# Loading half of q over SyncE's queue in fp32 at the start of a pooled-attention and gated-projection kernel

## The chip, the core and the metric

The kernel runs on one core of a Trainium2 chip. The metric is the time of one execution on the device in microseconds (us), as the median of several executions. The traces used here are of one profiled execution of each kernel; their span runs from the first to the last instruction and is some 1.8 us shorter than the time. All times in the text without another origin are counted from the start of that span.

## The reference

```python
# q, k, v: [8, 8, 576, 64] fp32 (batch, head, token, depth)
k_p = k.reshape(B, H, Sp, 8, D).mean(axis=3)           # 576 keys pooled to 72
v_p = v.reshape(B, H, Sp, 8, D).mean(axis=3)
attn = softmax(q @ k_p.transpose(0, 1, 3, 2) / sqrt(D))
x = (attn @ v_p).transpose(0, 2, 1, 3).reshape(4608, 512)
h = x @ w_in                                           # [512, 2048]
out = (h * cos(h)) @ w_out                             # [2048, 512]
```

## The kernel before

The two big products run in nine chunks of 512 tokens, and attention of the later batches is woven into them. Only batch 0 has nothing to hide under: its k, q and v must be loaded, pooled on TensorE (a product with a 0/1 matrix called `groups`), transposed, and go through softmax, before the first big product can start. The start looks like this (cut):

```python
warm = consts.tile([128, 512], BF16, name="warm")
nc.vector.memset(warm, 1.0)
...
# half of k in fp32 over SyncE's queue, cast by ScalarE; the rest over GpSimd's queue, which casts as it loads
nc.sync.dma_start(out=k_first..., in_=even_view(k, 0, 0, 2))
nc.scalar.copy(out=staged["k", 0][:, 0:2]..., in_=k_first)
load_even(staged["q", 0], 0, q, 0, 2)          # GpSimd's queue: first half of q
... # GpSimd: index fills
load_even(staged["k", 0], 0, k, 2, 4)
load_even(staged["q", 0], 0, q, 2, 4)
load_even(staged["v", 0], 0, v)
make_identity(nc, identity)
... # VectorE: groups; then GpSimd: the weights, batch 1, w_out piece by piece

warm_up(10, obanks[0])                          # products that only keep TensorE's clock up
pool_k_mm(0, obanks[1], 0, 2)(vec)              # pool k's first half, VectorE copies it to kk
warm_up(2, banks[1][:, 0, :])
puts = q_transpose_mm(0, banks[2][:, 0, :], 0, 5), q_transpose_mm(0, obanks[0], 5, 9)
puts[0](vec)
puts[1](act)
warm_up(2, banks[1][:, 0, :])
scores(0, us[0], banks[0])
scores(0, us[1], banks[1])
... # second half of k and q, scores, v, sums and products with v
up_mm(0, 0, 0, 2)                               # first big product
```

Three moments carry the argument. The *first scores* need pooled k and transposed q. The *last scaled product* is the last of four by which VectorE finishes batch 0; TensorE's big products run without a gap from then on. And the *second piece* of w_out must have landed when TensorE comes to it at about 38 us.

The softmax here doesn't subtract the row's maximum and nothing guards it: scores larger than these inputs give would overflow.

## Time and profile before

The median of three executions was 303.98 us (303.52 to 304.59).

| moment, before | us |
|---|---|
| q's first half landed (issued from 1.26) | 7.05 |
| TensorE at full clock from | 6.51 |
| first scores start | 8.80 |
| last scaled product of batch 0 starts | 18.24 |
| second piece of w_out lands | 38.06 |
| TensorE takes it up, after a wait of 0.46 | 38.10 |
| last copy of a whole output tile (128x512) by VectorE | 294.88 |
| span | 302.1 |

In a line of the timeline the first two numbers are the start and the busy time in us; a bracket at the end gives how long the engine was idle before, and what ended that. In the chain of waits a line is start, duration, and what the end of the program was waiting for at that time. In the stretches, each engine has its busy time and, in brackets, its instructions, in the order PE, PEld, DVE, ACT, POOL; then come the granted TensorE clock (1.00 is full), the DMA share and GB/s written.

### The profile page before, as it was taken

Reading aid. Unit: us, or ns where it says so; the run is one execution under the profiler, and the core shown is the slowest. Engines: PE = TensorE matmul, PEld = TensorE weight load, DVE = VectorE, ACT = ScalarE, POOL = GpSimd, SP = SyncE. Lnnn points to the kernel's source line nnn. Section 1 sums busy time; section 2 is a strip of 40 time slices with the busy share of each in tenths; the row PEclk is TensorE's granted clock in tenths of the full one; section 3 lists DMA queues with packets and bytes.
Section 4 is the critical chain, followed back from the end, with each engine's and each line's share of the span. In section 5 each row is a group of like instructions: output and inputs, shape, how many; then the busy total and the mean of one; then the engine's idle time right before and its main releaser. Section 6 shows DMA issues by size and latency. Waiting matters only on the chain.

```text
span 302.1 us, 4605 instructions
## 1 busy us (share of the span) xinstructions
PE 294.0 (97%) x1798; PEld 141.6 (47%) x1798; DVE 172.3 (57%) x211; ACT 206.8 (68%) x255; POOL 129.8 (43%) x92
## 2 busy tenths in 40 slices
PE   8799999999999999999999999999999999999995
PEld 3545544445544454455444544454444544444444
DVE  5558636574566366645675566656574567425712
ACT  3887897469856986688768876788578956606500
POOL 8553007984973596349733991399100000000000
PEclk9999999999999999999999999999999999999999
DMA  7999999639546943695169617881900330131032
GB/s 152 201 207 206 208 204 196 152 44 174 109 113 105 167 92 70 123 171 113 44 132 161 115 36 162 129 141 36 167 5 1 71 69 0 27 79 35 0 71 71
DMA packets 44006, 32.92 MB, mean 109 GB/s; under 512 B 22096, under 2 KB 39248, under 8 KB 43984
## 3 DMA queue, kind: packets, MB, share of 16 engines
q0 software_dynamic: 19744, 18.07, 38.2%
q1 hardware_dynamic: 24080, 14.42, 21.0%
q8 instruction: 14, 0.23, 0.3%
q10 hardware_dynamic: 160, 0.13, 0.2%
q14 instruction: 8, 0.07, 0.1%
HBM read 36.70 MB, written 9.44 MB: 153 GB/s over the span
## 4 chain that ended last, share of the span: by engine, by line
PE 85%; DMA 10%; POOL 2%; ACT 1%; issue 0%; DVE 0%; POOLq 0%; ACTq 0%
PE obank L310 39%; PE bank L297 37%; DMA w_out_sb<-in_moe_w_out_dram 6%; PE bank L241 5%; DMA w_in_sb<-in_moe_w_in_dram 4%; PE bank L211 3%; PE bank L328 1%; POOL kv_st L84 1%; POOL kp L384 1%; POOL q_b L84 1%; ACT L285 0%; ACT cos L304 0%; ACT ex L218 0%; POOL identity masks.py:197 0%; DVE o_sb L316 0%
## 5 line engine op out<-in xcount | busy, mean ns | idle before, releaser
L310 PE MATMUL obank<-w_out_sb,g_sb 128*128 128x512 bf16 x560 | 132.5, 380 | 0.5 <-DMA w_out_sb<-in_moe_w_out_dram 0.5
L297 PE MATMUL bank<-xT,w_in_sb 128*128 128x512 bf16 x576 | 126.5, 379 | 0.0
L304 ACT ACTIVATE cos<-bank,half_pi 128x1024 f32<-128x1024 f32 x72 | 80.0, 1113 | 63.3 <-PE bank L297 63.3
L307 DVE TENSOR_TENSOR g_sb<-bank,cos 128x1024 bf16<-128x1024 f32 x72 | 88.1, 1225 | 48.2 <-ACT cos L304 48.2
L297 PEld LDWEIGHTS <-w_in_sb 128*128 128x128 bf16 x576 | 55.5, 98 | 68.6 <-DVE xT L252 2.5
L310 PEld LDWEIGHTS <-g_sb 128*128 128x128 bf16 x560 | 52.2, 97 | 56.9 <-issue 3.7
L252 DVE TENSOR_TENSOR xT<-bank,inv 64x512 bf16<-64x512 f32 (+1 forms) x72 | 45.3, 629 | 50.1 <-ACT inv L248 49.2
L141 POOL TENSOR_TENSOR kv_st<-kv_st 72x2048 f32<-72x2048 bf16 x12 | 48.7, 4056 | 35.2 <-DMA kv_st<-in_k_dram 35.2
L247 ACT ACTIVATE lnc<-bank 64x512 f32<-64x512 f32 (+1 forms) x72 | 39.2, 544 | 2.9 <-PE bank L241 1.3
L218 ACT ACTIVATE ex<-bank 72x1024 bf16<-72x1024 f32 (+1 forms) x40 | 35.0, 928 | 5.3 <-PE bank L211 5.2
L316 DVE COPY o_sb<-obank 128x512 f32<-128x512 f32 x35 | 23.6, 689 | 16.8 <-PE obank L310 16.2
L142 POOL TENSOR_TENSOR kv_st<-kv_st 72x1024 f32<-72x1024 f32 x12 | 28.2, 2348 | 1.0
L248 ACT ACTIVATE inv<-lnc 128x512 f32<-128x512 f32 (+1 forms) x36 | 21.0, 583 | 1.1
L241 PE MATMUL bank<-ex,vz 72*128 72x256 bf16 (+1 forms) x176 | 20.0, 243 | 0.2 <-ACT ex L218 0.2
L241 PEld LDWEIGHTS <-vz 72*128 72x128 bf16 x176 | 13.7, 97 | 9.9 <-issue 0.6
L145 POOL TENSOR_TENSOR kp<-kv_st 72x512 bf16<-72x512 f32 x12 | 14.9, 1264 | 0.5
L211 PE MATMUL bank<-qT,kk 64*72 64x256 bf16 (+1 forms) x192 | 13.3, 252 | 1.1 <-ACT qT L193 0.5
L211 PEld LDWEIGHTS <-kk 64*72 64x72 bf16 x192 | 7.6, 110 | 11.9 <-issue 8.1
L285 ACT ACT_TABLE_LOAD x9 | 11.5, 1283 | 0.9 <-PEq L515 0.7
L288 ACT ACT_TABLE_LOAD x9 | 11.5, 1283 | 0.2
L495 POOL COPY gate<-kk 1x1 bf16<-1x1 bf16 x5 | 0.9, 180 | 24.7 <-DMA kk<-kp 24.7
L84 POOL DMA_DIRECT2D q_b<-in_q_dram x10 | 7.7, 773 | 2.7 <-DMA w_in_sb<-in_moe_w_in_dram 1.4
(55 smaller groups left out, 89.8 us busy)
## 6 DMA issues: line engine op xcount, KB each, us to landing
out_dram<-o_sb SPq DMA_DIRECT2D x70, 128.0 KB, 2.4
kv_st<-in_v_dram POOLq DMA_DIRECT2D x8, 576.0 KB, 13.0
kv_st<-in_k_dram POOLq DMA_DIRECT2D x7, 576.0 KB, 7.7
q_b<-in_q_dram POOLq DMA_DIRECT2D x6, 576.0 KB, 9.9
w_in_sb<-in_moe_w_in_dram POOLq DMA_DIRECT2D x4, 512.0 KB, 13.7
w_out_sb<-in_moe_w_out_dram POOLq DMA_DIRECT2D x4, 512.0 KB, 18.4
q_b<-in_q_dram POOLq DMA_DIRECT2D x4, 288.0 KB, 12.1
g_sb<-in_k_dram SPq DMA_DIRECT2D x1, 576.0 KB, 3.5
```

Source lines behind the costliest of these rows:

```text
L141: add(out=s, in0=x[:, :, 0:4, :], in1=x[:, :, 4:8, :], op=ADD)
L142: add(out=s[:, :, 0:2, :], in0=s[:, :, 0:2, :], in1=s[:, :, 2:4, :], op=ADD)
L211: nc.tensor.matmul(pair[:Sp, bank, c:c + n].rearrange("p (g n) -> p g n", n=64), lhsT=kk[b % 2][half[r], h0 + i, 0:Sp], rhs=att["qT", b][h ...
L218: nc.scalar.activation(out=ex[:, 0:nh * n].rearrange("p (a n) -> p a n", a=2), in_=pair[:Sp, :, 0:nh * n // 2], func=ACTF.Exp, scale=scale ...
L241: nc.tensor.matmul(pair[:, hp, (i // 2) * n:(i // 2 + 1) * n], lhsT=vz[b % 2][:, pj, 2 * hp:2 * hp + 2, :].rearrange("p a d -> p (a d)"), ...
L247: nc.scalar.activation(out=lnc[half[1 - hp]], in_=pair[half[1 - hp], hp, 0:w], func=ACTF.Ln)
L252: nc.vector.tensor_mul(out=x_out(b, u, half[hp]), in0=cols(pair[half[hp], hp, :], u), in1=cols(inv[half[1 - hp]], u))
L297: nc.tensor.matmul(h[:, j, :], lhsT=w_in_sb[fc // 4][:, ki, (fc % 4) * 128:(fc % 4 + 1) * 128], rhs=xT[:, ki, t * TILE:(t + 1) * TILE], st ...
L304: nc.scalar.activation(out=cos, in_=h, func=ACTF.Sin, bias=half_pi[:, :1])
L307: nc.vector.tensor_mul(out=g_sb[:, 2 * fp:2 * fp + 2, :], in0=h, in1=cos)
L310: nc.tensor.matmul(o, lhsT=g_sb[:, fc, ms * 128:(ms + 1) * 128], rhs=w_out_sb[fc // 4][:, fc % 4, :], start=(fc == 0), stop=(fc == FFCH - 1))
L316: nc.vector.tensor_copy(out=o[:, 0:n], in_=ps)
```

## The change

The intent is to feed batch 0 sooner. k's half comes in two loads, one per pair of heads, so that its cast starts on the first. q's half goes the same way over SyncE's queue in fp32, instead of over GpSimd's queue, and VectorE casts it. v comes in two loads, pooled and copied apart. Each product gets a PSUM bank tile of its own, so that the copies out can be shared between VectorE and ScalarE. The warm-up tile is smaller, and there are eight first warm-ups, not ten. The core of the diff (the pooling functions that take a list of banks, and batch 1's matching calls, are cut):

```diff
-    warm = consts.tile([128, 512], BF16, name="warm")
+    warm = consts.tile([128, 128], BF16, name="warm")
...
-    k_first = g_sb...[:, 0:2 * ROW * D]
-    nc.sync.dma_start(out=k_first..., in_=even_view(k, 0, 0, 2))
-    nc.scalar.copy(out=staged["k", 0][:, 0:2]..., in_=k_first)
-    load_even(staged["q", 0], 0, q, 0, 2)
+    for i, (which, src) in enumerate((("k", k), ("q", q))):
+        for j in range(2):
+            first[which, j] = g_sb...[:, (2 * i + j) * n:(2 * i + j + 1) * n]
+            nc.sync.dma_start(out=first[which, j], in_=even_view(src, 0, j, j + 1)...)
+    for j in range(2):
+        cast_first("k", nc.scalar.copy, j)
...
-    load_even(staged["v", 0], 0, v)
+    load_even(staged["v", 0], 0, v, 0, 2)
+    load_even(staged["v", 0], 0, v, 2, 4)
...
-    warm_up(10, obanks[0])
-    pool_k_mm(0, obanks[1], 0, 2)(vec)
-    warm_up(2, banks[1][:, 0, :])
+    warm_up(8, obanks[0])
+    puts = pool_k_mm(0, obanks, 0, 2)
+    for j in range(2):
+        cast_first("q", vec, j)
+    puts[0](act)
+    puts[1](vec)
+    warm_up(1, banks[2][:, 0, :])
...
+    for put in pool_k_mm(0, [banks[1][:, i, :] for i in range(2)], 2, 4):
+        put(vec)
     sums_first(0, us[1], obanks[1])
+    for put in [q_transpose_mm(0, banks[0][:, i, :], 9 + 5 * i, 14 + 4 * i) for i in range(2)]:
+        put(vec)
+    pool_v_mm(0, obanks, 0, 2)
+    scores(0, us[2], banks[2])
+    scores(0, us[3], banks[1])
+    values_then(0, us[0], obanks[0])
+    values_then(0, us[1], obanks[1])
+    pool_v_mm(0, (banks[0][:, 0, :], banks[0][:, 1, :]), 2, 4)
+    sums_first(0, us[2], banks[2][:, 0, :])
+    sums_first(0, us[3], banks[1][:, 0, :])
```

More of the change, by code (lines that the diff above doesn't have):

```diff
@@ L126, in v_part @@
         return vz[b % 2][:, :, 0:4:3, :]
-    def put_kk(b, ps, pj0, pj1, copy):
-        dst = kk[b % 2].rearrange("p (j a) n -> p j a n", a=2)
-        for a in range(2):
-            for r in range(2):
-                copy(out=dst[half[r], pj0:pj1, a, 0:Sp], in_=ps[half[a]])
     def pool_add(b, which):
@@ L148, in pool_add, with pool_k_mm, put, go @@
             add(out=v_part(b), in0=s[..., 0, :], in1=s[..., 1, :], op=ADD)
-    def pool_k_mm(b, bank, pj0, pj1):
+    def pool_k_mm(b, ps, pj0, pj1):
         kb = staged["k", b]
-        ps = bank[:, 0:(pj1 - pj0) * Sp].rearrange("p (j n) -> p j n", n=Sp)
+        ps = [p[half[a], 0:(pj1 - pj0) * Sp].rearrange("p (j n) -> p j n", n=Sp) for a, p in enumerate(ps)]
         for pj in range(pj0, pj1):
             for t in range(ROW):
-                for rows in half:
-                    nc.tensor.matmul(ps[rows, pj - pj0, :], lhsT=kb[rows, pj, t, :], rhs=groups[rows, t, :],
+                for a in range(2):
+                    nc.tensor.matmul(ps[a][:, pj - pj0, :], lhsT=kb[half[a], pj, t, :], rhs=groups[half[a], t, :],
                                      start=(t == 0), stop=(t == ROW - 1))
-        return lambda copy: put_kk(b, ps, pj0, pj1, copy)
-    def pool_v_mm(b, pair):
+        dst = kk[b % 2].rearrange("p (j a) n -> p j a n", a=2)
+        def put(a):
+            def go(copy):
+                for r in range(2):
+                    copy(out=dst[half[r], pj0:pj1, a, 0:Sp], in_=ps[a])
+            return go
+        return put(0), put(1)
+    def pool_v_mm(b, ps, pj0=0, pj1=KCH):
         vb = staged["v", b]
+        ps = [p[:Sp, 0:(pj1 - pj0) * D] for p in ps]
         for t in range(ROW):
             for hp, rows in enumerate(half):
-                nc.tensor.matmul(pair[:Sp, hp, 0:KCH * D], lhsT=groups[rows, t, :], rhs=vb[rows, :, t, :],
+                nc.tensor.matmul(ps[hp], lhsT=groups[rows, t, :], rhs=vb[rows, pj0:pj1, t, :],
                                  start=(t == 0), stop=(t == ROW - 1))
-        nc.vector.tensor_copy(out=v_part(b).rearrange("p j a d -> p a j d"),
-                              in_=pair[:Sp, :, 0:KCH * D].rearrange("p a (j d) -> p a j d", j=KCH))
+        for hp in range(2):
+            nc.vector.tensor_copy(out=v_part(b)[:, pj0:pj1, hp, :], in_=ps[hp].rearrange("p (j d) -> p j d", d=D))
     def k_transpose(b):
@@ L340, with cast_first @@
     q_tile(0)
-    k_first = g_sb.rearrange("p f n -> p (f n)").bitcast(FP32)[:, 0:2 * ROW * D]
-    nc.sync.dma_start(out=k_first.rearrange("p (j n) -> p j n", j=2), in_=even_view(k, 0, 0, 2))
-    nc.scalar.copy(out=staged["k", 0][:, 0:2].rearrange("p j t d -> p (j t d)"), in_=k_first)
-    load_even(staged["q", 0], 0, q, 0, 2)
+    first = {}
+    n = ROW * D
+    for i, (which, src) in enumerate((("k", k), ("q", q))):
+        for j in range(2):
+            first[which, j] = g_sb.rearrange("p f n -> p (f n)").bitcast(FP32)[:, (2 * i + j) * n:(2 * i + j + 1) * n]
+            nc.sync.dma_start(out=first[which, j], in_=even_view(src, 0, j, j + 1).rearrange("p j n -> p (j n)"))
+    def cast_first(which, copy, j):
+        copy(out=staged[which, 0][:, j].rearrange("p t d -> p (t d)"), in_=first[which, j])
+    for j in range(2):
+        cast_first("k", nc.scalar.copy, j)
     row_of = consts.tile([128, ROW], FP32, name="row_of")
@@ L360 @@
     groups = consts.tile([128, ROW, Sp], BF16, name="groups")
-    nc.vector.tensor_tensor(out=dist, in0=row_of.unsqueeze(2).to_broadcast([128, ROW, Sp]),
-                            in1=first_of.unsqueeze(1).to_broadcast([128, ROW, Sp]), op=mybir.AluOpType.subtract)
-    nc.vector.scalar_tensor_tensor(out=sign, in0=dist, scalar=1.0 - POOL, in1=dist, op0=ADD,
-                                   op1=mybir.AluOpType.mult)
-    nc.vector.tensor_scalar(out=groups, in0=sign, scalar1=0.0, scalar2=None, op0=mybir.AluOpType.is_le)
     nc.vector.memset(vz[0], float(POOL))
@@ L371 @@
     nc.vector.memset(half_pi, math.pi / 2.0)
+    nc.vector.tensor_tensor(out=dist, in0=row_of.unsqueeze(2).to_broadcast([128, ROW, Sp]),
+                            in1=first_of.unsqueeze(1).to_broadcast([128, ROW, Sp]), op=mybir.AluOpType.subtract)
+    nc.vector.scalar_tensor_tensor(out=sign, in0=dist, scalar=1.0 - POOL, in1=dist, op0=ADD,
+                                   op1=mybir.AluOpType.mult)
+    nc.vector.tensor_scalar(out=groups, in0=sign, scalar1=0.0, scalar2=None, op0=mybir.AluOpType.is_le)
     kv_even_tiles(1)
@@ L382 @@
     load_even(staged["v", 1], 1, v)
+    nc.gpsimd.memset(vz[1], float(POOL))
     for i in range(2):
@@ L390, in warm_up @@
         for i in range(n):
-            nc.tensor.matmul(bank, lhsT=warm[:, 0:128], rhs=warm)
+            nc.tensor.matmul(bank.rearrange("p (a n) -> p a n", a=4), lhsT=warm,
+                             rhs=warm.unsqueeze(1).to_broadcast([128, 4, 128]))
     vec, act = nc.vector.tensor_copy, nc.scalar.copy
     us = BY_HEADS
-    warm_up(10, obanks[0])
-    pool_k_mm(0, obanks[1], 0, 2)(vec)
-    warm_up(2, banks[1][:, 0, :])
-    puts = q_transpose_mm(0, banks[2][:, 0, :], 0, 5), q_transpose_mm(0, obanks[0], 5, 9)
+    warm_up(8, obanks[0])
[5 more added lines that the diff above has]
+    warm_up(1, banks[2][:, 0, :])
+    puts = q_transpose_mm(0, banks[1][:, 0, :], 0, 5), q_transpose_mm(0, banks[0][:, 0, :], 5, 9)
     puts[0](vec)
     puts[1](act)
-    warm_up(2, banks[1][:, 0, :])
-    scores(0, us[0], banks[0])
-    scores(0, us[1], banks[1])
-    pool_k_mm(0, obanks[1], 2, 4)(vec)
-    sums_first(0, us[0], banks[0][:, 0, :])
-    puts = q_transpose_mm(0, banks[2][:, 0, :], 9, 14), q_transpose_mm(0, obanks[0], 14, 18)
-    puts[0](vec)
-    puts[1](act)
-    sums_first(0, us[1], obanks[1])
-    scores(0, us[2], banks[0])
-    scores(0, us[3], banks[2])
-    nc.vector.memset(vz[1], float(POOL))
-    pool_v_mm(0, banks[1])
-    sums_first(0, us[2], obanks[0])
-    values_then(0, us[0], obanks[1])
-    values_then(0, us[1], banks[1][:, 0, :])
-    sums_first(0, us[3], banks[2][:, 0, :])
-    values_then(0, us[2], obanks[1])
-    values_then(0, us[3], obanks[0])
+    warm_up(2, banks[2][:, 0, :])
+    scores(0, us[0], banks[2])
+    scores(0, us[1], banks[0])
+    sums_first(0, us[0], obanks[0])
+    for put in pool_k_mm(0, [banks[1][:, i, :] for i in range(2)], 2, 4):
+        put(vec)
+    sums_first(0, us[1], obanks[1])
+    for put in [q_transpose_mm(0, banks[0][:, i, :], 9 + 5 * i, 14 + 4 * i) for i in range(2)]:
[8 more added lines that the diff above has]
+    sums_first(0, us[3], banks[1][:, 0, :])
+    values_then(0, us[2], obanks[0])
+    values_then(0, us[3], obanks[1])
     up_mm(0, 0, 0, 2)
@@ L431 @@
                 if fp == 4:
-                    puts = pool_k_mm(1, obanks[0], 0, 2), pool_k_mm(1, obanks[1], 2, 4)
+                    puts = pool_k_mm(1, obanks, 0, 4)
                 elif fp in (5, 6):
@@ L464 @@
         if t == 0:
-            fill[1:] = [(2, S_(0, 0)), (8, lambda: pool_v_mm(1, banks[1])), (8, lambda: values(t, REST, banks[2])),
+            fill[1:] = [(2, S_(0, 0)), (8, lambda: pool_v_mm(1, [banks[1][:, i, :] for i in range(2)])), (8, lambda: values(t, REST, banks[2])),
                         (11, S_(1, 0)), (13, V_(0, 1)), (18, S_(2, 2)), (21, V_(1, 0, later)), (26, S_(3, 1)),
```

## The prediction

> **What bounds the kernel now.** I read four views in this order: the page (busy shares, slices, the chain by engine), the chain of waits in order of time for the first 60 us, the timeline of the first 20 us, and the stretches by microsecond. The page first:
>
> ```profile
> PE 294.0 (97%) x1798; PEld 141.6 (47%) x1798; DVE 172.3 (57%) x211; ACT 206.8 (68%) x255; POOL 129.8 (43%) x92
> ...
> PE   8799999999999999999999999999999999999995
> ...
> GB/s 152 201 207 206 208 204 196 152 44 174 109 113 105 167 92 70 123 171 113 44 132 161 115 36 162 129 141 36 167 5 1 71 69 0 27 79 35 0 71 71
> ...
> PE 85%; DMA 10%; POOL 2%; ACT 1%; issue 0%; DVE 0%; POOLq 0%; ACTq 0%
> ```
>
> TensorE is busy 97% of the span and carries 85% of the chain; only the first two of the 40 slices (15 us) are short of 9 tenths before the end. The change touches batch 0 and, slightly, batch 1's product in chunk 0, so it can win no more than what is lost at the start. But DMA holds 10% of the chain, and the transfers run flat out at some 207 GB/s from slice 1 to slice 5 (38 us). So where do these DMA pieces lie? The chain in order of time:
>
> ```profile
> 5.81 10.94 DMA w_in_sb<-in_moe_w_in_dram
> ...
> 19.62 18.43 DMA w_out_sb<-in_moe_w_out_dram
> 38.06 0.04 issue
> 38.10 0.81 PE obank L310 x3
> ```
>
> From 5.81 to 38.06 us the chain is not batch 0's work at all: it is the weights in GpSimd's queue. A piece of the second projection's weights, issued at 19.62, lands at 38.06, and TensorE waits for it. From 38.10 on the chain is TensorE alone. The timeline shows how small that wait is, and the beginning and end of batch 0:
>
> ```profile
> 1.26 0.87 POOL L84 DMA_DIRECT2D q_b<-in_q_dram  x1 [0.81 <-POOLq L515]
> 1.47 4.45 PE L391 MATMUL obank<-warm 128*128 128x512 bf16 x10 [1.47 <-DVE warm L336]
> 4.30 1.15 ACT L343 CAST kv_st<-g_sb 128x1152 bf16<-128x1152 f32 x1 [2.27 <-DMA g_sb<-in_k_dram]
> 5.84 1.06 PE L157 MATMUL obank<-groups,kv_st 64*64 64x72 bf16 x36
> 8.80 0.63 PE L211 MATMUL bank<-qT,kk 64*72 64x256 bf16 x8 [0.43 <-DVE qT L193]
> 13.86 1.91 ACT L218 ACTIVATE ex<-bank 72x1024 bf16<-72x1024 f32 x2
> 18.24 0.69 DVE L282 TENSOR_TENSOR xT<-obank,inv 128x512 bf16<-128x512 f32 x1 [0.50 <-ACT inv L271]
> 38.10 0.81 PE L310 MATMUL obank<-w_out_sb,g_sb 128*128 128x512 bf16 x3 [0.46 <-DMA w_out_sb<-in_moe_w_out_dram]
> ```
>
> So batch 0's scores start at 8.80, its last product is scaled until 18.93, TensorE is then dense, and at 38.10 it has lost 0.46 us to the weights. The stretches by microsecond show the transfers starting badly (last column GB/s, before it the DMA share):
>
> ```profile
> 3.00:4.00 1.00, 1.00 (x3) 0.29 (x2) 0.96 (x2) 0.00 (x0) 1.00 (x2) 1.00 1.12 327
> 4.00:5.00 1.00, 1.00 (x4) 0.43 (x3) 0.96 (x2) 0.70 (x1) 1.00 (x2) 1.00 0.82 97
> 5.00:6.00 1.00, 1.00 (x9) 0.16 (x9) 0.84 (x2) 0.45 (x1) 0.93 (x4) 1.00 1.11 167
> 6.00:7.00 1.00, 1.00 (x37) 0.90 (x36) 0.56 (x4) 0.00 (x0) 1.00 (x2) 1.00 1.19 182
> 7.00:8.00 1.00, 1.00 (x13) 0.69 (x11) 0.94 (x4) 0.02 (x1) 1.00 (x2) 1.00 1.12 179
> 8.00:9.00 1.00, 0.57 (x6) 0.30 (x6) 0.72 (x2) 0.57 (x1) 1.00 (x3) 1.00 1.16 179
> ```
>
> SyncE's fp32 load of k runs in 2 to 4 us; then it is over, and GpSimd's queue, whose casting loads write half of what they read, comes up slowly: 97, 167, 182, 179, 179 against 207 later. That is 110+40+25+28+28 = 231 KB written short, or 231/207 = 1.1 us of transfer time lost. This, not the engines' work, sets when the weights land.
>
> **What the Trainium skill says.** "DMA: Bandwidth & Descriptors", section "Issuing engines are not separate DMA queues": all queues feed the same 16 engines and interleave, and several issuers save only issue time. The trace agrees as far as it goes: one queue alone holds the share above 1. The same page, "Latency and other measured facts", gives the first byte after about 600 ns on the hardware path and about 1 us on GpSimd's. In the packet records SyncE's load issued at 0.75 to 1.21 sends its first packet at 1.86, 0.65 us after the issue; GpSimd's, issued at 1.26 to 2.13, at 3.74, 1.6 us after. So SyncE agrees and GpSimd is slower than the page. "TensorE: Matmul & The Clock Gate", section "What's actually happening": the array runs at half clock until it has been busy for about 3.4 us; here the ten warm-up products cost 4.45/10 = 0.445 us each, and four later ones 0.60/2 = 0.30 or less. "PSUM — Partial Sum Buffer", section "PSUM bank collisions raise a hardware error": engines must be kept apart by bank and quadrant. That is the reason for a bank tile per product; no collision was allowed before either, so it buys independence of the two copies, not speed of the products.
>
> **The change part by part.**
>
> *Start of TensorE.* The warm-up tile shrinks from 128x512 to 128x128: its fill, 0.48 us, falls to about 0.15, so warm-up starts near 1.15 instead of 1.47. Eight at 0.445 take 3.6: done near 4.75. The two halves of k land near 3.5 and 4.3, and each casts on ScalarE in about 1.15/2 = 0.6: done at 4.1 and 4.9. The group matrix needs three VectorE operations (0.83+0.83+0.74 = 2.4 us); a fill of v's tile now stands before them, but GpSimd's index fills come first by 0.8 us, so they run 2.2 to 4.65. Pooling k's first half starts near 4.8, not 5.84: 1.0 us won, unless the array is still at half clock, which doubles 1.06 us and gives most of it back.
>
> *q's first half.* Two fp32 loads on SyncE behind k, 256 packets at k's pace (0.59 MB at some 390 GB/s = 1.5 us), shared with GpSimd's queue from about 4.2: landing near 5.4 and 6.4. Two new casts on VectorE of 128x576; by the 745 ns of the group compare on 648 elements, about 0.66 each: done near 6.1 and 7.05. Then VectorE's share of the copies of pooled k falls from four (1.28 us) to two (0.65), as ScalarE does the other two: done at 7.7, and the copy of q's transpose (0.49) at 8.2. Scores start near 8.2 against 8.80: 0.6 won. The casts eat 0.4 of the 1.0.
>
> *Rest of batch 0.* ScalarE is the bound from 9.25 to 18.21, with hardly a gap. One 0.57 us copy of q's transpose goes to VectorE. But the second two heads' pairs now wait on VectorE: four copies of k (1.26) and two of q's transpose (0.49+0.43) after a pooling which ends near 10.7: 10.7+2.2 = 12.9, scores 12.95, exponentials from 13.3 instead of 13.86. Four operations of normalising follow as before; the last scaled product is ready at about 18.4, not 18.93. v in two halves lies under this: half the columns, same 18 products a half, and two short copies instead of one of 0.69. **TensorE's gain at the start: 0.5 us.**
>
> *The transfers.* Bytes read are the same. A fp32 packet of SyncE (2304 B) takes 93 ns in the records; a casting one (1152 B written) takes 107, but these overlap by a share of 1.2, so about 89 each; 256 packets over 16 engines differ by 16 x 4 ns, under 0.1 us. What is won is that q's packets fill 4.0 to 5.6 us, where 110+30 KB are missing (0.7 us). Against it GpSimd's first load is issued after the index fills, some 0.6 us later, so part of its slow start moves to 5 to 9 us. **Net about 0.6 us earlier for every later landing.** GpSimd's extra fill (0.91 us, ahead of the second piece of those weights) delays an issue, not the landing: that piece waits 18.4 us behind some six others.
>
> *Sum at the wait of 38.10.* TensorE arrives at 37.64-0.5 = 37.1; the weights at 38.06-0.6 = 37.45. It starts at 37.5: 0.6 won. The next two pieces landed at 40.60 and 43.10 (18.4 and 18.1 us after issues at 22.16 and 24.96) against needs near 40.9 and 43.5; both move alike and stay just in time. After that TensorE alone counts and nothing has changed. The gain is the smaller of 0.5+0.46 (TensorE) and about 0.6 (transfers): 303.98-0.6 = 303.4; I say 303.3, as the transfers' gain could reach 1.1.
>
> **The rivals.**
>
> 1. *Full gain at the start.* If all 1.0 us of the earlier pooling reached the end, and the DMA followed, 302.9. For it: the chain's first 6 us. Against: the casts on VectorE, and the wait at 38.10.
> 2. *Transfers not advanced.* If GpSimd's slow start only moves later, the weights still land at 38.06 and TensorE waits 0.9 us instead of 0.46: 304.0, nothing won. For it: GpSimd's rate is below 207 up to 9 us whatever SyncE does, and its first load starts later.
> 3. *Harm.* SyncE's packets delay GpSimd's loads of k and q for the other heads, or the array is cold after eight warm-ups; scores slip 0.5 to 1 us: but the 0.46 of slack absorbs half: 304.5.
>
> I give these 25, 25 and 10%, and the central story 40.
>
> **Range and chances.** The rivals span 302.9 to 304.5, and the three runs of before spread over 1.1 us. Range 302.4 to 304.3. 2% is 6.1 us, three times what is lost between 1.5 and 19 us by any count above, so faster by over 2% has 1%, slower 1%, within 98%.
>
> **What would show each step.** Warm-up's start (1.15), first pooling (4.8), first scores (8.2), last scaled product of batch 0 (18.4), DMA rate at 4 to 6 us (over 200), landing of the second piece of the second weights (37.45) and TensorE's wait before it (0.3 to 0.5). If scores come a microsecond early and the end doesn't, rival 2 holds and the landing will still be 38. If the landing moves by over 1 us, I undersized the transfers. A slot of TensorE idle after 50 us that wasn't there before would prove me wrong: I take that phase as unchanged.

## The result, and the profile after

The changed kernel took 308.16, 308.17, 308.92 and 308.45 us, median 308.31; the kernel before took 303.98, 304.59, 303.52 and 303.52 in the same rounds, median 303.75. The ratio is 1.0149, with a 95% interval of 1.0124 to 1.0174. That is inside the 2% called the same, but clear: 4.6 us slower, and outside the predicted range. (A ratio here compares mean times of the same rounds, so it is not quite the ratio of the medians.)

From the page of the changed kernel, the share of TensorE and its clock in 40 slices of 7.7 us, and the chain by engine:

```profile
PE   6599999999999999999999999999999999999994
...
PEclk9589999999999999999999999999999999999999
...
PE 92%; DMA 2%; ACT 2%; issue 1%; DVE 1%; SPq 0%; ACTq 0%
```

Before, the first two digits of PE were 8 and 7. Now the second slice has 5 of TensorE and also 5 of its clock. The chain has lost most of its DMA, 10% to 2%, so the wait for the weights is not what sets the end any more. What the chain now runs through at the start is this:

```profile
2.14 7.41 DMA g_sb<-in_q_dram
9.57 0.47 DVE q_b L355
...
10.09 0.71 PE bank L197 x5
...
12.27 1.03 ACT ex L223
...
22.85 0.70 DVE xT L287
23.59 7.10 PE bank L302 x32
```

Everything waits for a load of q that SyncE began to issue at 2.14 and that landed at 9.54. It was predicted at 6.4. The timeline answers the lines that the prediction showed of before:

```profile
1.07 3.59 PE L407 MATMUL obank<-warm 128*128 128x512 bf16 x8 [1.07 <-DVE warm L341]
...
4.59 0.96 PE L152 MATMUL obank<-groups,kv_st 64*64 64x72 bf16 x36
...
6.61 0.46 DVE L355 CAST q_b<-g_sb 128x576 bf16<-128x576 f32 x1 [2.30 <-DMA g_sb<-in_q_dram]
7.13 0.40 PE L197 MATMUL bank<-identity,q_b 128*128 128x128 bf16 x4 [1.26 <-DVE q_b L355]
...
9.57 0.46 DVE L355 CAST q_b<-g_sb 128x576 bf16<-128x576 f32 x1 [2.50 <-DMA g_sb<-in_q_dram]
10.09 0.71 PE L197 MATMUL bank<-identity,q_b 128*128 128x128 bf16 x5 [2.56 <-DVE q_b L355]
...
11.58 1.07 PE L216 MATMUL bank<-qT,kk 64*72 64x256 bf16 x8
...
22.85 0.69 DVE L287 TENSOR_TENSOR xT<-obank,inv 128x512 bf16<-128x512 f32 x1 [0.60 <-ACT inv L276]
...
42.08 0.81 PE L315 MATMUL obank<-w_out_sb,g_sb 128*128 128x512 bf16 x3
```

The reader should see four things. The warm-up and the pooling of k start early, as planned (1.07 and 4.59). The second cast of q waits 2.50 us for its load, and TensorE 2.56 us behind it. The eight products of the first scores take 1.07 us where they took 0.63 before: the clock. And the product at 42.08 has no bracket: the weights had long been there.

The stretches of two microseconds show the hole and the clock that follows it:

```profile
6.00:8.00 2.00, 0.40 (x4) 0.23 (x4) 0.46 (x1) 0.15 (x1) 2.00 (x3) 1.00 1.02 199
8.00:10.00 2.00, 0.00 (x0) 0.00 (x0) 0.43 (x1) 0.00 (x0) 0.47 (x2) 0.52 1.17 199
10.00:12.00 2.00, 1.91 (x11) 1.04 (x13) 1.14 (x4) 0.58 (x1) 1.10 (x2) 0.50 1.21 205
```

TensorE works 0.40 us of the 4 us from 6 to 10. In the records its clock is full from 4.67 to 8.08, half from 8.08 to 18.32, and full from there to the end of the work. Meanwhile the transfers are not idle (199 GB/s), so I asked whose packets they are. The packets of each queue, in 4.5 to 7.5 us of the changed kernel (q0 is GpSimd's, q1 SyncE's; packets, MB written, share of 16 engines):

```profile
q0 software_dynamic: 277, 0.31, 77.0%
q1 hardware_dynamic: 135, 0.27, 27.0%
```

The same in 8 to 10 us of the changed kernel:

```profile
q0 software_dynamic: 335, 0.37, 111.9%
q1 hardware_dynamic: 18, 0.03, 4.9%
```

And in 4.5 to 7.5 us of the kernel before, where GpSimd's queue was alone:

```profile
q0 software_dynamic: 448, 0.49, 107.1%
```

While SyncE's queue had the engines to itself, from 2.0 to 4.3 us, it moved 365 packets. GpSimd's first packet is recorded at 4.31. After that SyncE's packets come at 135 in 3 us, and the last 18 trickle in between 8 and 10 us beside 335 of GpSimd's. SyncE's queue slowed when GpSimd's packets appeared at 4.31 (194 of its packets in 3 to 4 us, 25 in 5 to 6), not when GpSimd began to issue its loads at 1.42. The two queues together made 412 packets from 4.5 to 7.5, against 448 of GpSimd's queue before; but there GpSimd's queue had started 0.57 us earlier (3.74). Counted for 3 us from GpSimd's first packet, it is 421 packets of both queues in the changed kernel (156 of them SyncE's) and 402 in the kernel before (25). So in these two traces the two queues together do not move fewer packets than one; what changed is whose packets go.

The moments side by side, with four of the experiments that follow:

| | before | after | filled clock | fills first | identity first | fills, reordered |
|---|---|---|---|---|---|---|
| first half of q complete | 7.05 | 9.54 | 10.21 | 6.74 | 6.74 | 5.97 |
| first scores start | 8.80 | 11.58 | 11.93 | 8.46 | 8.46 | 7.69 |
| last scaled product starts | 18.24 | 22.85 | 21.69 | 18.22 | 18.22 | 18.69 |
| from scores to there | 9.44 | 11.27 | 9.76 | 9.76 | 9.76 | 11.00 |
| second piece of w_out lands | 38.06 | 38.11 | 39.51 | 38.40 | 37.88 | 37.69 |
| TensorE takes it up | 38.10 | 42.08 | 40.92 | 38.44 | 37.92 | 37.93 |
| of that, wait | 0.46 | 0 | 0 | 0.82 | 0.30 | 0 |
| last copy of a whole output tile | 294.88 | 298.88 | 297.74 | 295.24 | 294.72 | 294.74 |
| span | 302.1 | 306.4 | 305.2 | 302.7 | 302.2 | 302.2 |

All copies of finished output tiles, from the first at 44.84 against 48.82 to the last, lie 3.98 to 4.01 us later than before. So all of this arises before the first copy, and the long dense part is unchanged; some 0.3 us more come after the last copy.

### The profile page after: what moved, and what is told of

The parts are those of the page before. It is cut to its first block, busy times and chain, and to the rows that moved or that the text cites. A ratio compares the mean times of both kernels' runs of the same rounds, so it can differ in the third digit from the quotient of the medians.

```text
span 306.4 us, 4647 instructions
## 1 busy us (share of the span) xinstructions
PE 296.0 (97%) x1813; PEld 143.1 (47%) x1813; DVE 171.3 (56%) x213; ACT 206.8 (68%) x255; POOL 130.6 (43%) x93
## 3 DMA queue, kind: packets, MB, share of 16 engines
HBM read 36.70 MB, written 9.44 MB: 151 GB/s over the span
## 4 chain that ended last, share of the span: by engine, by line
PE 92%; DMA 2%; ACT 2%; issue 1%; DVE 1%; SPq 0%; ACTq 0%
PE bank L302 40%; PE obank L315 39%; PE bank L246 5%; PE bank L216 4%; DMA g_sb<-in_q_dram 2%; PE bank L333 1%; ACT ex L223 1%; PE bank L197 1%; PE obank L152 0%; ACT L290 0%; ACT inv L276 0%; SPq L352 0%; PE bank L152 0%; ACT lnc L275 0%; PE obank L271 0%
## 5 line engine op out<-in xcount | busy, mean ns | idle before, releaser
L290 ACT ACT_TABLE_LOAD x9 | 11.5, 1283 | 0.9 <-PEq L536 0.7
L293 ACT ACT_TABLE_LOAD x9 | 11.5, 1283 | 0.2
L103 POOL DMA_DIRECT2D kv_st<-in_v_dram x6 | 5.1, 842 | 12.7 <-PE bank L170 12.7
```

## The experiments

The first theory: q's second load is late because GpSimd's packets share the 16 engines with it, and the idle time this makes costs TensorE its clock on top. The rivals: the place of the load in SyncE's queue or its splitting is to blame; or the new compute order and the bank tiles are; or the warm-up is too short. A fourth question is why the change would not have gained even with q in time. Twelve kernels ran, all with correct results, on four chips; each call timed the kernel before on the same chip.

One thing disturbs the intervals. Some executions of the kernel before take 307.1 to 307.7 us with a mean clock of 0.983 to 0.989: 3 of 7 on the first chip, 2 of 11 on the second, none of 11 on the third (one of 305.15) and 1 of 11 on the fourth. They are not marked as slow, as none is 1.5% above the fastest, and they widen the ratios.

### q's half back on GpSimd's queue

```diff
-    for i, (which, src) in enumerate((("k", k), ("q", q))):
+    for i, (which, src) in enumerate((("k", k),)):
...
+    load_even(staged["q", 0], 0, q, 0, 2)
...
-    for j in range(2):
-        cast_first("q", vec, j)
```

> The change with one part undone: the first half of q goes back to GpSimd's casting queue, first in it, ahead of the index fills; the two casts on VectorE go. Theory A (the whole loss is q's second fp32 load, which landed at 9.54 us instead of the predicted 6.4): q lands near 7.0 as in the kernel before, the scores start near 8.1 instead of 11.58, the end is at 303.0 to 303.8 us. Rival B (the loss is in the reordered products and copies, or in v's two loads): 306 us or more though q lands early.

Measured: 304.10, 304.49, 304.45, 303.68, median 304.28; before in the same rounds 303.57 to 304.3 in four executions and 307.14 to 307.73 in three; ratio 0.9972 (0.9898 to 1.0045). q's half landed at 7.41, the first scores started at 9.38, and the last scaled product at 19.16. So this one part of the change, q's path, holds nearly the whole loss of the time: with all the rest in place the kernel is back within some 0.5 us of the four shorter executions of before. The scores are still 0.58 later than before; here q's half landed 0.36 later, eight warm-ups ended 0.68 us before `groups` was ready, the clock was full only from 9.46, and pooling took 1.29 us instead of the 0.96 of the changed kernel. The wait of 0.46 us for the weights absorbed most of that.

### Warm-up products over the wait

```diff
-    warm_up(1, banks[2][:, 0, :])
+    warm_up(18, banks[2][:, 0, :])
```

> The changed kernel with 18 warm-up products instead of 1 between the pooling of k and the transposes of q, so that TensorE is busy while it waits for q and its clock should not fall to half. The loads are untouched: q's second half should land near 9.5 as in the changed kernel. Theory C (a part of the 4.0 us is the half clock from 8.1 to 18.3): scores near 10.9, last scaled product near 21.2 instead of 22.85, end near 306.7 (1.3 to 1.8 less than the changed kernel's 308.3). Rival D (the record of the clock is not to be trusted, as one of the four timed runs shows 1.0 at the same span): no gain, 308.3 within 0.3.

Measured: 307.02, 306.25, 306.73, 307.01, median 306.87; ratio 1.0053 (0.9965 to 1.0142). The clock was full from 4.13 us on. From the timeline of this kernel:

```profile
11.93 0.63 PE L216 MATMUL bank<-qT,kk 64*72 64x256 bf16 x8 [0.30 <-DVE qT L198]
...
21.69 0.69 DVE L287 TENSOR_TENSOR xT<-obank,inv 128x512 bf16<-128x512 f32 x1 [0.60 <-ACT inv L276]
```

The scores take 0.63 us again, and the way from the scores to the last scaled product is 21.69 - 11.93 = 9.76 us, against 22.85 - 11.58 = 11.27 with half the clock. So the half clock cost 1.5 us of that way. q's loads landed late here too (8.64 and 10.21), so the lateness does not come from what TensorE does. This kernel is still some 3 us behind before: the load is the larger part.

### GpSimd's fills ahead of its loads

```diff
+    nc.gpsimd.memset(vz[1], float(POOL))
+    identity = consts.tile([128, 128], BF16, name="identity")
+    make_identity(nc, identity)
     load_even(staged["k", 0], 0, k, 2, 4)      # first of GpSimd's loads
```

> The changed kernel with GpSimd's fills (v's tile of batch 1 and the identity, about 1.4 us) ahead of its first load instead of behind, so that its queue begins near 5.7 us instead of 4.31, when SyncE's four loads should be through. Theory E (SyncE's packets are crowded out once GpSimd's queue is filled): q's two loads land near 4.8 and 5.4, scores start near 8.0, and the weights land later by up to 1 us: end 303.6 to 304.8. Rival F (SyncE's fourth load is late on its own, whatever GpSimd does): q's second half lands at 9 us or later, the end is 308 or more.

Measured: 304.54, 304.15, 304.03, 305.17, median 304.35; ratio 0.9981 (0.9907 to 1.0056). Nothing on SyncE's side was touched; GpSimd's first load was only issued at 3.02 instead of 1.42. From the timeline:

```profile
3.02 0.88 POOL L84 DMA_DIRECT2D kv_st<-in_k_dram  x1
...
6.05 0.46 DVE L355 CAST q_b<-g_sb 128x576 bf16<-128x576 f32 x1 [1.74 <-DMA g_sb<-in_q_dram]
6.76 0.46 DVE L355 CAST q_b<-g_sb 128x576 bf16<-128x576 f32 x1 [0.26 <-DMA g_sb<-in_q_dram]
8.46 0.63 PE L216 MATMUL bank<-qT,kk 64*72 64x256 bf16 x8 [0.30 <-DVE qT L198]
```

q landed at 6.03 and 6.74, 2.80 us earlier than in the changed kernel, and the clock stayed full. This is the clearest run: the same loads in the same queue land that much earlier when GpSimd issues its first load 1.6 us later (its first packet came at 5.11 instead of 4.31). The last scaled product began at 18.22, 0.02 before that of the kernel before. But the second piece of w_out landed 0.34 later (38.40), so TensorE waited 0.82 us for it, and nothing was won.

### The compute part of the change alone

```diff
-        for j in range(2):
-            first[which, j] = ...
-            nc.sync.dma_start(out=first[which, j], ...)
+        k_first = ...
+        nc.sync.dma_start(out=k_first..., in_=even_view(k, 0, 0, 2))
...
-    load_even(staged["v", 0], 0, v, 0, 2)
-    load_even(staged["v", 0], 0, v, 2, 4)
+    load_even(staged["v", 0], 0, v)
```

(against the first experiment: k and v too are loaded as before)

> The change without any of its loads: k's half in one load and one cast, q's half on GpSimd first, v in one load, as in the kernel before; the products in bank tiles of their own, the order of the products, the smaller warm-up tile and the moved fills stay. If the compute part is worth something by itself: scores near 8.2, end 303.2 to 303.7 (the weights land at 38.06 as before and hold the gain to 0.46). If it is harmful: 304.5 or more.

Measured: 304.31, 304.41, 304.57, 304.18, median 304.36; ratio 0.9978 (0.9905 to 1.0051). Scores at 9.46, last scaled product at 19.31, TensorE at the weights at 38.55. It stands as the first experiment does, 0.1 us behind: the halves of k and v make no difference that can be seen, and the compute part does not do the harm.

### Only the identity ahead of the loads

```diff
+    identity = consts.tile([128, 128], BF16, name="identity")
+    make_identity(nc, identity)
     load_even(staged["k", 0], 0, k, 2, 4)
```

> The changed kernel with only the identity's two fills (about 0.55 us) moved ahead of GpSimd's first load: a small dose of the run with all fills first (1.6 us, q landed at 6.03 and 6.74). GpSimd's queue should send its first packet near 4.85 instead of 4.31. If SyncE's packets are crowded out from the moment GpSimd's queue sends, what is left of them at that moment shrinks from 165 of 576 to about 105, and q's second half lands between, near 8.0 us, the end between 304.4 and 307.5. If there is a threshold instead (the queue late on its own, or only by the identity): 9.0 or later, or 6.8.

Measured: 304.01 and 304.45; before 303.40 to 304.08 in nine executions and 307.37 and 307.38 in two; ratio 0.9992 (0.9908 to 1.0075). I had meant this as a half dose of the delay, and it was not one. From the timeline:

```profile
1.65 1.41 POOL masks.py:199 TENSOR_SCALAR_AFFINE_SELECT identity<-identity 128x128 bf16<-128x128 bf16 x1
3.01 0.88 POOL L84 DMA_DIRECT2D kv_st<-in_k_dram  x1
```

The select took 1.41 us here, beside VectorE's work, and 0.29 us in its old place (why, no run shows), so the load left at 3.01, as in the run above. The landings of q and the start of the scores are the same to 0.01 us (6.03 and 6.74, 8.46), which confirms that run with one fill less. With the weights at 37.88 instead of 38.40, the span was 302.2, against 302.1 before.

### q's second load from ScalarE

```diff
+            issuer = nc.scalar if (which, j) == ("q", 1) else nc.sync
-            nc.sync.dma_start(out=first[which, j], ...)
+            issuer.dma_start(out=first[which, j], ...)
```

> The changed kernel with q's second half-load issued on ScalarE's queue, behind its table load, at about the same time (2.0 us) as on SyncE's. If the second half is late because it stands fourth in SyncE's queue (rival G), it lands by 7 us now, and q's first half by 6. If every packet of the hardware queues is crowded out once GpSimd's queue sends (theory E), a second hardware queue helps only by its own share of turns: it lands near 7.5 to 8.5. If that share does not exist, at 9 or later.

Measured: 307.60 and 305.92; ratio 1.0075 (0.9988 to 1.0162). The rival was that the fourth place in SyncE's queue is what is late. The views of transfers by issue (KB, us from issue to landing):

```profile
g_sb<-in_q_dram ACTq DMA_DIRECT2D x1, 288.0 KB, 3.4
...
g_sb<-in_q_dram SPq DMA_DIRECT2D x1, 288.0 KB, 6.8
```

ScalarE issued its load at 0.79, earlier than I had expected (2.0), and it landed at 4.22. But now q's first half, the last in SyncE's queue, was the late one, at 8.50. Scores at 10.96, the clock half from 7.13 to 17.37, the last scaled product at 22.23. Three of four loads got out before GpSimd's packets; whichever came last paid. So this load is not special. Nor is it simply the amount still to come when GpSimd's packets start that decides. From GpSimd's first packet on, SyncE's queue had 74 packets left here, and its last load landed at 8.50; with the fills first it had 87 left, and 6.74; with q as one load (told next) 247, and 7.84. What the landings do go with is when GpSimd issues its first load: at 1.42 q's last load on SyncE lands at 7.84 to 10.21 (four traces), at 1.88 at 7.87, at 3.01 or 3.02 at 5.97 to 6.74 (three traces).

### q's half as one load

```diff
+    q_first = g_sb...[:, 2 * n:4 * n]
+    nc.sync.dma_start(out=q_first..., in_=even_view(q, 0, 0, 2))
```

(in place of the two loads of q)

> The changed kernel with q's half as one load of 0.59 MB on SyncE instead of two by head pair; two casts as before. Theory E: bytes and start are the same, so the whole lands at 9 to 10 us and the end is 308 to 309. Rival H (the loss comes of issuing by head pair: four loads on the queue, each with its own end): it lands by 7.5, the end is 305 or less.

Measured: 306.26 and 308.91; ratio 1.0102 (1.0011 to 1.0193). The one load landed at 7.84, later than with the fills first and earlier than in the changed kernel. In the profiled execution GpSimd's packets also started slowly: 1, 2, 11 and 38 in the half microseconds from 3.5. Scores at 9.94, half clock from 9.29 to 16.11, last scaled product at 21.18. Splitting is therefore not the cause, since the unsplit load is late too; whether a single load suffers less, or GpSimd merely started slower in this execution, one trace does not tell.

### Half the delay

```diff
+    for i in range(2):
+        nc.gpsimd.memset(kp2[i][:, 0:2], 0.0)
     load_even(staged["k", 0], 0, k, 2, 4)
...
-        nc.gpsimd.memset(kp2[i], 0.0)
+        nc.gpsimd.memset(kp2[i][:, 2:], 0.0)
```

> The dose that the run with the identity first was meant to give and did not (there GpSimd's first load was issued at 3.01 instead of 1.42, the same 1.6 us as with all fills first, as the identity's select took 1.41 us beside VectorE's work): two small fills of about 0.25 us each ahead of GpSimd's first load, which should go out near 1.9 and send its first packet near 4.8. Theory E (what SyncE has left when GpSimd's queue begins to send is crowded out): q's second half lands between 6.74 and 9.54, near 8; the end at 304.5 to 307.5. If q lands at 9.5 or at 6.7 as in one of the two, it is a threshold and not a remainder.

Measured: 306.13 and 307.69; before 303.33 to 304.40 in ten executions, and one of 305.15; ratio 1.0096 (1.0062 to 1.0130). GpSimd issued its first load at 1.88, and its first packets came at 5.0 to 5.5. q landed at 5.44 and 7.87: between 9.54 (load issued at 1.42) and 6.74 (at 3.02). Counted by the issue, a dose in between gave an effect in between in this execution. Counted by GpSimd's first packet it was no dose in between (5.21, against 4.31 and 5.11), and the other execution, 307.69, is close to the changed kernel's times. One trace is not the whole story here: the same loads landed at 9.54 and 10.21 in two traces (changed kernel, filled clock), and at 6.74 and 5.97 in two others (fills first, last run). Scores at 9.60; the clock was half for two of the 3.41 us steps (8.91 to 15.74) instead of three.

### The kernel before with the small parts that looked good

```diff
-    warm = consts.tile([128, 512], BF16, name="warm")
+    warm = consts.tile([128, 128], BF16, name="warm")
...
-    warm_up(10, obanks[0])
-    pool_k_mm(0, obanks[1], 0, 2)(vec)
+    warm_up(11, banks[0][:, 0, :])
+    puts = pool_k_apart(0, obanks, 0, 2)
+    puts[0](act)
+    puts[1](vec)
```

> The kernel before, with two parts of the change alone: the smaller warm-up tile (TensorE starts near 1.07) with 11 warm-up products so that no gap stands before the first pooling, and k's first pooled product in two bank tiles, copied by ScalarE and VectorE apart. Loads and the order of the products are those of the kernel before. Scores near 8.3 instead of 8.80; the weights still land near 38.06, so at most 0.46 us can be won: 303.3 to 303.8 where the clock is full. If the slow executions of the kernel before (307.1 to 307.7, three of seven in the last rounds) come from a clock that falls in its first 20 us, fewer of them here than of the kernel before in the same rounds.

Measured: 303.95, 303.39, 307.50, 303.64, 303.72, 307.89, median 303.83; ratio 1.0025 (0.9954 to 1.0095). The scores came 0.21 earlier than before (8.59), but the last scaled product did not (18.30 against 18.24), and the weights landed at 38.13. Nothing is won, and two of its six executions were among the slower ones, so it does not cure those either.

### The other way round: all of k on SyncE, q first on GpSimd

```diff
-    load_even(staged["k", 0], 0, k, 2, 4)
+    for j in (2, 3):
+        at = g_sb...[:, j * ROW * D:(j + 1) * ROW * D]
+        nc.sync.dma_start(out=at, in_=even_view(k, 0, j, j + 1)...)
```

(on top of the kernel just told; VectorE casts these two)

> The finding turned round: what is urgent goes to the queue that does the crowding. From the run with k's product in apart tiles (loads as before): the other half of k goes over SyncE in fp32 too, by head pair, cast on VectorE, and q's first half is GpSimd's first load. Theory E: q lands near 7.2 as before, k's late half is crowded out and lands at 7.5 to 9, which the scores do not need; GpSimd has 0.59 MB less to bring before the weights, so the second piece of the second projection's weights lands near 37.5 instead of 38.06, and the end is at 303.0 to 303.6 where the clock is full. If k's late half lands after 9.5, scores of the second half slip and the end is 304 or more.

Measured: 306.60, 305.54, 304.75, 305.56, 305.05, 305.21, median 305.37; ratio 1.0048 (1.0027 to 1.0068). I had expected this to help, as what the scores need first would be on the queue that had won in the changed kernel. It did not. From the view of transfers by issue:

```profile
q_b<-in_q_dram POOLq DMA_DIRECT2D x1, 288.0 KB, 8.2
```

The same load took 5.8 us from issue to landing in the kernel before. It landed at 9.50, and k's last load on SyncE at 9.09. In the kernel just told, without k's second half on SyncE, it had landed at 7.50. In 4.5 to 7.5 us there were 232 packets of GpSimd's queue and 126 of SyncE's. So the crowding is not one-sided: here the overlap held back GpSimd's load too. I had thought of GpSimd's queue as the one that always wins; that idea fell here.

### The kernel before, cold

```diff
-    warm_up(10, obanks[0])
+    warm_up(0, obanks[0])
```

> The kernel before without its first ten warm-up products, so that TensorE is idle until about 5.5 us and runs the first part of batch 0 at half clock. This measures what the clock costs by itself with the loads untouched. If the slow executions of the kernel before (307.1 to 307.7, five of eighteen so far, granted clock 0.983 to 0.989) are a lost clock and nothing else, this kernel stands at 305.5 to 307.7 in every execution, with a clock near 0.98; if the half clock costs only what TensorE's share of the chain in batch 0 says (under 1.5 us), at 304.5 to 305.5.

Measured: 304.35, 304.32, 303.68, 304.33, median 304.32; ratio 1.0003 (0.9980 to 1.0027). The clock was full only from 11.5 us, the scores came at 9.61 (0.81 late), the last scaled product at 19.33 (1.09 late), and TensorE reached the weights at 38.56, 0.46 late. Early cold products are cheap here because the wait for the weights takes up much of it. It is the long half clock in the middle of batch 0 that costs. The run also shows that a missed warm-up does not explain the executions of 307 us.

### The change with GpSimd's fills first and scores ahead of v

```diff
-    warm_up(1, banks[2][:, 0, :])
+    warm_up(3, banks[2][:, 0, :])
...
-    pool_v_mm(0, obanks, 0, 2)
     scores(0, us[2], banks[2])
     scores(0, us[3], banks[1])
+    pool_v_mm(0, obanks, 0, 2)
```

(against the kernel with GpSimd's fills first)

> The best version the runs point to: the changed kernel with GpSimd's fills ahead of its first load (q landed at 6.03 and 6.74 so), the scores of the second two head pairs ahead of v's first product (they waited 0.45 us behind it), and three warm-up products instead of one before the transposes of q. Scores near 8.4, last scaled product of batch 0 near 17.8 instead of 18.22. If the weights' landing caps the gain, as predicted, TensorE waits longer for them near 38 us and the end is that of the fills-first run and of the kernel before: 303.6 to 304.4, verdict same. If batch 0 counted in full, 0.4 us less than the fills-first run, clearly below the kernel before.

Measured: 304.01, 306.21, 304.51, 304.41, 304.68, 304.24, median 304.46; before 303.57 to 304.11 in ten executions and one of 307.27; ratio 1.0022 (0.9982 to 1.0063). In this execution q landed even sooner (5.97), the scores started at 7.69, 1.11 before those of before, and the weights landed at 37.69. Yet TensorE came to the weights at 37.93, later than with the old order (37.62, which is the 37.92 of the run with the identity first, less its wait of 0.30). ScalarE's timeline, in this kernel:

```profile
16.11 0.60 ACT L275 ACTIVATE lnc<-bank 128x512 f32<-128x512 f32 x1 [1.04 <-PE bank L271]
```

and in the run with the identity first:

```profile
13.73 1.93 ACT L223 ACTIVATE ex<-bank 72x1024 bf16<-72x1024 f32 x2 [0.46 <-PE bank L216]
```

With the old order ScalarE idles 0.46 us before the second exponentials and goes on without a gap. With the new order it idles 0.64 before them and then 1.04 more, because the sums that it needs stand on TensorE behind v's products. The head start of over a microsecond went into these waits. No kernel beat the kernel before.

## Why the prediction was wrong

**The step that failed first is the landing of q's half**, in the paragraph "q's first half": "landing near 5.4 and 6.4". It landed at 6.59 and 9.54. The working took 256 packets at SyncE's pace and let them be "shared with GpSimd's queue from about 4.2" as if that cost little. With GpSimd's loads held back by 1.6 us, the same loads land at 6.03 and 6.74, and in the last run at 5.06 and 5.97, on both sides of 5.4 and 6.4. So the sum without sharing was about right, and the sharing, 2.8 to 3.6 us for the second load, was the missing term. I had seen that GpSimd's queue would run from 4.2; I had rival 3 for it, "SyncE's packets delay GpSimd's loads", with the roles exchanged, a size of 0.5 to 1 us, and a chance of 10%. The Trainium skill's page "DMA: Bandwidth & Descriptors", section "Queues, rings and completion order", says that each engine takes turns between the queues that have work, a packet at a time. Even sharing of the measured total of 412 in 3 us would have given SyncE's queue 206 packets from 4.5 to 7.5; 165 were left, so it would have been done by about 6.9 (an estimate). The records show 135, and 18 more in 8 to 10. The pieces that the records count need not be the page's packets, so the runs do not refute its rule; they show that even sharing was not what came out of it. From q's landing the rest follows: the scores began 1.72 us after it in the kernels with filled clock, fills first and identity first, at full clock (1.73 in the half dose), and I had put 1.8; in the changed kernel, at half clock, it was 2.04.

**A term that the sum did not have is the clock.** Rival 3 had "the array is cold after eight warm-ups", which did not happen in the changed kernel's trace: the clock was full from 4.67, 0.08 us after pooling began. (It did in the runs with q's half back on GpSimd's queue and with the compute part alone: full only from 9.46 and 9.67, pooling 1.29 us.) What I did not think of is that a late load makes TensorE idle, and this takes the clock away afterwards. The clock changes in the records at intervals of 3.41 us, and in these traces a fall goes with TensorE's busy time in the step before it. In the changed kernel (first line) and with q's second load from ScalarE (second), the clock fell at the end of these steps:

```profile
4.67:8.08 3.41, 1.60 (x41) 0.99 (x41) 0.46 (x1) 0.89 (x3) 3.33 (x6) 1.00 1.05 189
```

```profile
3.72:7.13 3.41, 1.82 (x40) 0.86 (x38) 0.56 (x2) 1.89 (x4) 3.33 (x7) 1.00 1.04 241
```

With the identity first it stayed full after this one:

```profile
6.28:9.69 3.41, 2.07 (x20) 1.19 (x20) 1.80 (x5) 1.61 (x3) 3.41 (x5) 1.00 1.05 141
```

Busy 1.82 us or less of 3.41 lost the clock (1.25 and 1.37 in the runs with one load and half the delay, 1.64 with all of k on SyncE); 2.07 or more kept it (2.46 with fills first, 2.98 before). No step of the fourteen traces breaks this while the products run; where between 1.82 and 2.07 the border lies, none shows. In the changed kernel it came back only after a step that was busy throughout, at 18.32, three steps later. The experiment with filled clock puts this at 1.5 us.

**The gain at the start was not there either.** "TensorE's gain at the start: 0.5 us" rested on scores at 8.2 and a last product at 18.4. The two runs with GpSimd's loads held back and the order of the change had scores at 8.46, 0.34 before those of before, and took 9.76 us from there instead of 9.44, so TensorE came to the weights at 37.62 against 37.64. I had expected second exponentials at 13.3; they came at 13.73. The new order gives up 0.3 us that the earlier start had won.

**The transfers were not advanced.** "Net about 0.6 us earlier for every later landing" was wrong and rival 2 was right in this: w_out's second piece landed at 38.11 (before 38.06), and in the runs with GpSimd held back at 37.88 and 38.40. The sign that I had named came true all the same: 224 GB/s written in 4 to 6 us, where it had been 132. But GB/s written was the wrong measure. A packet of SyncE's fp32 load writes 2304 B, one of a casting load 1152 B, so the rate rises when q changes queue without more packets going: from 4 to 8 us there were 576 packets of both queues, and 571 before. (Over all runs with q or k on SyncE that piece landed anywhere from 37.10, with half the delay, to 39.51, with the filled clock, so single traces do not settle a gain of 0.6.)

The account of the loss: scores 2.78 later (11.58 - 8.80); from there to the last scaled product 1.83 more (11.27 - 9.44), of which 1.5 is the clock and 0.3 the order; together 4.61. The wait of 0.46 us for the weights is gone, and 0.17 more is absorbed before the dense part: 3.98 at the first output tile and at the last. With 0.3 in the tail the span is 4.3 longer.

What was right: warm-up from 1.07 (predicted 1.15), pooling at 4.59 (4.8), k's loads at 3.72 and 4.32 (3.5 and 4.3), casts of q somewhat cheaper than reckoned (0.46 each against 0.66), a dense part that does not change, and that the weights at 38 cap any gain: with q in time, in the runs with the fills or the identity first, the time was that of before, not better. The range was built on rivals of which none had a loss over 0.5 us, and at 304.3 it even left out the third rival's own 304.5; a load moved to another queue deserved a larger loss.

**Left open.** How the DMA engines divide their time between the two queues, and why SyncE's last packets trail so long, no run shows; that the overlap with GpSimd's loads makes q late is shown, the rule of sharing is not. Nor what makes the executions of before at 307 us: none was profiled. The 0.3 us after the last copy appears in several kernels that load q by SyncE, and is not explained. One of the four executions of the changed kernel recorded a mean clock of 1.0 at the same span of 306.4; I have no trace of it.

## What to carry to other kernels

A load moved to another queue is not moved out of the way: ask which transfers will be under way beside it when its last packets are due, and hold back those that are needed later (here a delay of 1.6 us at GpSimd brought q 2.8 us forward). Count a late load twice where TensorE has nothing else to do: once for the wait, and again for the clock that it loses, unless some products fill the gap. And before advancing a start, look for the next thing that the same time will wait for; here the weights at 38 us left 0.46 us to win.

## What the Trainium skill lacked or had wrong

- "DMA: Bandwidth & Descriptors", section "Issuing engines are not separate DMA queues": it lacks what the overlap can cost. SyncE's queue went from 365 packets in 2.3 us to 135 in 3 us once GpSimd's packets began, and a 288 KB load ended at 9.54 with GpSimd's first load issued at 1.42, and at 6.74 with it issued at 3.02.
- The same page, "Queues, rings and completion order": taking turns by packet does not let one foresee the shares. The records showed 277 to 135 pieces in 3 us, then 335 to 18, all that SyncE's queue had left, in 2 us, so the end of a short load can trail far behind.
- The same page, "Latency and other measured facts": its first byte of about 1 us for GpSimd's queue was 2.0 us after the end of the first issue in the changed kernel (2.29 to 4.31), 1.6 before, and 1.2 with the fills first (3.90 to 5.11).
- "TensorE: Matmul & The Clock Gate", section "HAM oscillation — how this bites in real kernels": it warns of idle gaps over about 3.4 us. Here the longest gap between products was 2.56 us and the clock had already fallen before it ended; steps of 3.41 us with 1.25 to 1.82 us busy lost it, steps with 2.07 to 2.98 kept it. The length of the step, 3.41 us, agrees with the page.
